# One maximum for both halves of a query's keys, and 1/sum applied to the attention's output

## The chip, the cores and the metric

The kernel runs on one core of a Trainium2 chip. The metric is the device time of one execution in microseconds, as the median of several runs. A profile of one execution gives a trace: when each instruction started and ended on each engine. TensorE (PE, with its weight loads PEld), VectorE (DVE), ScalarE (ACT), GpSimd (POOL) and the DMA queue of SyncE (SP) work side by side and wait for each other by semaphores.

## The reference

Block-causal attention over 8 batches, 8 heads, 576 positions and 64 dimensions, followed by a gated feed-forward layer with a depthwise convolution:

```python
scores = (q @ k^T) / 8
scores = where(pos_i // 64 >= pos_j // 64, scores, -1e9)
attn = exp(scores - max(scores, axis=-1))
attn = attn / (sum(attn, axis=-1) + 1e-9)
x = attn @ v                       # heads side by side: [8, 576, 512]
h = relu(x @ w_in)                 # w_in [512, 1024]
conv = sum over k of conv_w[k] * h shifted by k - 1      # 3 taps along the sequence
out = (h * sigmoid(conv)) @ w_out  # w_out [1024, 512]
```

All is float32. The kernel keeps the precision of the two large products by splitting each operand in a high and a low part (`x`: hi and lo, `wih`/`wil`, `woh`/`wol`, `gh`/`gl`), and runs three matmuls for each product.

## The kernel before

**Pairs and visits.** Attention works on pairs of heads, 32 pairs in all, four to a batch. The first batch is visited twice (part A: query blocks 0 to 3, part B: blocks 4 to 8), all other pairs once (part None, blocks 0 to 8), which makes 36 visits, here called pair 0 to 35. After the four pairs of a batch its feed-forward runs in two halves (`ffn`): first products on line 998, second products on line 1064.

**Scores.** A query block of 64 rows sees `b + 1` key blocks. The kernel lays a block's scores out so that the four quadrants of 32 partitions hold two groups of 32 queries times two halves of the keys: quadrants 0 and 1 (and 2 and 3) have the same queries and different halves of their keys. Only so do 64 queries fill 128 partitions. The blocks of a pair go in sets, `((8, 5), (7, 6), (4, 3, 2, 1, 0))`; each set takes two PSUM banks. TensorE makes the scores (line 852), VectorE the maximum of each row over its half (line 865, stored negated in `st`), ScalarE the exponential with that maximum as bias and the row sum as a by-product (line 870), all into `p`.

**Joining the halves.** Each half has its own maximum, so `merge` joins them: four copies of 32 partitions (ScalarE line 886 for two quadrants, GpSimd through the helper on line 506 for two) bring the other half's maximum and sum; then a subtraction (L893), an exponential of it (L896), two small operations (L899, L903) and a reciprocal (L907) give a factor for each row. GpSimd multiplies all of P with it (`norm`, line 919), in two operations for each block.

**PV.** VectorE transposes P in 32 x 32 blocks (line 938) into `ptw`, TensorE multiplies it with V (line 951, 144 matmuls in a full pair), and the output, transposed (dimensions on partitions, queries along the row), is evicted as a high part by ScalarE (line 965) and a low part by VectorE (line 968) straight from PSUM.

**Order.** Nothing is scheduled when the kernel is built: `Plan.op` numbers the operations, and the list `ORDER` gives the order in which they are issued, which is the order of each engine's queue, the DMA queue of SP included. `BANKS` says which PSUM bank each operation uses. `FILLS` puts filler matmuls (line 1159, `operation:bank:count`, result unused) ahead of named operations on TensorE. All three lists were computed beforehand from estimated costs of the operations; the numbers in the calls of `pl.op` (durations, target times) have no effect on the code that runs.

Of the kernel before, what the change touches and what calls it, by code (L numbers as in the profile page):

```python
# [195 lines left out]
"""  # L196

FILLS = """
46:0:17 32:0:9 62:0:2 127:0:6 58:0:17 257:4:4 165:3:10 566:0:7 28:2:14 391:6:2 295:0:5 495:3:2 431:5:1 755:0:7 719:0:6
# [995 lines left out]
```

## Time and profile before

| | |
|---|---|
| median of 3 runs | 693.44 us (692.34 to 694.99) |
| the profiled execution's own time | 692.34 us |
| its span (first to last instruction) | 690.2 us |
| mean granted TensorE clock | 0.998 |
| busy, share of the span | PE 97%, PEld 81%, DVE 84%, ACT 77%, POOL 65% |

The span is 2.1 us shorter than the time of the same execution. Matmuls are pipelined, so a busy TensorE is not one that works at its peak rate; how close it is shows in the time from one matmul to the next.

### The profile page before, as it was taken

To read this page: it belongs to the slowest core of one execution; us is meant where nothing else is said; L and a number is where in the kernel's file an instruction comes from. 1 tells how busy PE (TensorE), PEld (TensorE's weight loads), DVE (VectorE), ACT (ScalarE), POOL (GpSimd) and SP (SyncE) were. 2 spreads that over 40 slices of the span, in tenths; PEclk is the share of its full clock that TensorE was granted. 3 is DMA by queue.
4 is the path that set the end of the run, shared out by engine and by line. 5 is a ranking of instruction groups with operands and counts; after the bars stand their busy time and mean duration, and the time that the engine had idled before them with its cause. 6 is when DMAs were issued, how large, how long until landed. Compare 5 with 4: busy or idle time off the path is not lost.

```text
span 690.2 us, 29902 instructions
## 1 busy us (share of the span) xinstructions
PE 669.7 (97%) x12090; PEld 562.0 (81%) x12090; DVE 581.8 (84%) x1409; ACT 531.6 (77%) x2004; POOL 449.0 (65%) x918
## 2 busy tenths in 40 slices
PE   8979999999999999999999999999999999999998
PEld 6666768868979788887888889787988788888986
DVE  5778999998799878989799989988899978886662
ACT  5867888888798768887878879876789777884663
POOL 1564676886677955687668765778567765676242
PEclk9999999999999999999999999999999999999999
DMA  6885565417434342434343434424443352212002
GB/s 168 182 197 111 110 140 86 76 39 145 96 62 85 70 104 53 86 79 96 59 80 76 91 78 81 71 65 75 95 77 70 72 123 44 53 37 83 2 0 77
DMA packets 238542, 58.59 MB, mean 85 GB/s; under 512 B 228524, under 2 KB 232900, under 8 KB 238404
## 3 DMA queue, kind: packets, MB, share of 16 engines
q1 hardware_dynamic: 237060, 55.76, 39.5%
q8 instruction: 95, 1.56, 1.0%
q10 hardware_dynamic: 1344, 0.92, 0.4%
q14 instruction: 43, 0.35, 0.2%
HBM read 47.21 MB, written 9.44 MB: 82 GB/s over the span
## 4 chain that ended last, share of the span: by engine, by line
PE 72%; DVE 9%; ACT 6%; POOL 4%; issue 4%; DMA 2%; SPq 2%; DVEq 0%; POOLq 0%; ACTq 0%
PE banks L1064 25%; PE banks L998 24%; PE banks L951 11%; PE banks L852 10%; POOL p L919 3%; ACT p L870 3%; DVE ptw L938 2%; DVE st L865 2%; PE banks L691 1%; PE banks L1159 1%; SPq L538 1%; DMA t<-in_moe_conv_w_dram 1%; DVE t L1031 1%; ACT t L1015 1%; POOL gl L1038 1%
## 5 line engine op out<-in xcount | busy, mean ns | idle before, releaser
L919 POOL TENSOR_SCALAR p<-p,st 128x224 f32<-128x224 f32 (+8 forms) x576 | 262.9, 475 | 59.4 <-DVE st L907 52.2
L870 ACT ACTIVATE p<-banks,st 128x288 f32<-128x288 f32 (+8 forms) x576 | 220.6, 400 | 40.2 <-DVE st L865 27.5
L998 PE MATMUL banks<-x,wih 128*128 128x290 f32 (+3 forms) x1024 | 186.3, 301 | 1.2 <-ACT x L965 1.2
L998 PEld LDWEIGHTS banks<-x,wih 128*128 128x128 f32 x1024 | 154.8, 189 | 11.0 <-issue 3.0
L1038 POOL TENSOR_TENSOR gl<-t,gh 128x289 fp32r<-128x289 f32 (+3 forms) x128 | 106.4, 841 | 56.1 <-ACT gh L1035 45.7
L938 DVE STREAM_TRANSPOSE ptw<-p 128x576 f32<-128x576 f32 (+8 forms) x272 | 127.8, 495 | 12.8 <-POOL p L919 4.6
L865 DVE TENSOR_REDUCE st<-banks 128x2 f32<-128x64 f32 (+8 forms) x288 | 124.8, 471 | 12.0 <-PE banks L852 11.5
L870 ACT ACTIVATION_READ_ACCUMULATOR p<-banks,st 128x1 f32 x576 | 121.8, 211 | 0.0
L1064 PE MATMUL banks<-woh,gh 128*128 128x512 f32 (+1 forms) x296 | 119.0, 402 | 0.8 <-ACT h L1012 0.8
L1064 PE MATMUL banks<-woh,gl 128*128 128x512 f32 (+1 forms) x296 | 115.3, 389 | 0.3 <-POOL gl L1038 0.3
L1064 PE MATMUL banks<-wol,gh 128*128 128x512 f32 (+1 forms) x296 | 115.3, 390 | 0.0
L998 PE MATMUL banks<-x,wil 128*128 128x288 f32 (+3 forms) x512 | 105.8, 299 | 0.0
L852 PE MATMUL banks<-kT,qT 64*32 64x128 f32 (+8 forms) x4464 | 102.4, 302 | 3.2 <-issue 1.2
L852 PEld LDWEIGHTS banks<-kT,qT 64*32 64x32 f32 x4464 | 71.5, 105 | 31.4 <-issue 10.0
L951 PEld LDWEIGHTS banks<-ptw,vn 64*32 64x32 f32 x4608 | 81.1, 105 | 18.2 <-issue 5.4
L951 PE MATMUL banks<-ptw,vn 64*32 64x160 f32 (+8 forms) x4608 | 91.8, 296 | 4.2 <-issue 2.5
L1019 DVE SCALAR_TENSOR_TENSOR t<-h,cw,t 128x289 f32<-128x289 f32 (+3 forms) x128 | 74.8, 590 | 19.1 <-ACT t L1015 18.7
L506 POOL TENSOR_SCALAR st<-st 32x16 f32<-32x16 f32 (+2 forms) x136 | 34.0, 250 | 84.4 <-ACT p L870 32.1
L998 PEld LDWEIGHTS banks<-x,wil 128*128 128x128 f32 x512 | 82.1, 189 | 3.2 <-issue 1.1
L1023 DVE SCALAR_TENSOR_TENSOR t<-h,cw,t 128x288 f32<-128x288 f32 (+3 forms) x128 | 75.0, 594 | 1.6
L1015 ACT ACTIVATE t<-h,cw 128x289 f32<-128x289 f32 (+3 forms) x128 | 67.5, 536 | 5.9 <-POOL gl L1038 3.4
L1031 DVE SCALAR_TENSOR_TENSOR t<-t,h 128x289 f32<-128x289 f32 (+3 forms) x128 | 66.3, 529 | 5.7 <-ACT t L1028 5.1
(93 smaller groups left out, 797.2 us busy)
## 6 DMA issues: line engine op xcount, KB each, us to landing
vn<-in_v_dram SPq DMA_DIRECT2D x128, 144.0 KB, 3.6
out_dram<-stage SPq DMA_DIRECT2D x35, 256.0 KB, 2.6
kT<-in_k_dram SPq DMA_DIRECT2D x112, 72.0 KB, 3.0
qT<-in_q_dram SPq DMA_DIRECT2D x112, 72.0 KB, 2.9
x<-in_moe_w_out_dram SPq DMA_DIRECT2D x8, 512.0 KB, 4.8
gl<-in_moe_w_in_dram SPq DMA_DIRECT2D x4, 512.0 KB, 4.7
vxa<-in_v_dram SPq DMA_DIRECT2D x8, 128.0 KB, 5.3
gh<-in_moe_w_in_dram SPq DMA_DIRECT2D x2, 512.0 KB
```

What stands on the lines that cost most here:

```text
L852: nc.tensor.matmul(both(sb)[32 * quad:32 * quad + 32, h, o:o + w].rearrange("p (u n) -> p u n", n=32), t["q"].ap[r, 64 * b + 32 * g:64 * b ...
L865: nc.vector.tensor_reduce(out=st.ap[:, c:c + 2], in_=both(sb)[:, :, off:off + w], op=ALU.max, axis=AX.X, negate=True)
L870: nc.scalar.activation(out=pt.ap[:, h, :], in_=both(sb)[:, h, off:off + w], func=AF.Exp, bias=st.ap[:, c:c + 1], accum_out=st.ap[:, n + c: ...
L919: nc.gpsimd.tensor_scalar(out=pt.ap[:, h, :], in0=pt.ap[:, h, :], scalar1=st.ap[:, 5 * n + c:5 * n + c + 1], scalar2=0.0, op0=ALU.mult, op ...
L938: nc.vector.transpose(pt.ap[:, :, b:b + rise * b + 1:rise, :], x.ap.rearrange("p h (u n) -> p h u n", n=32))
L951: nc.tensor.matmul(both(vb)[o:o + 32, g, 32 * (lo - b0):32 * (b1 - b0)].rearrange("p (b n) -> p b n", n=32), vat(u, h)[r, 32 * y:32 * y + ...
L998: nc.tensor.matmul(fb.ap[:, 0:n2], wt[:, c, fs], xs[c][xi].ap[:, x0:x0 + n2], start=(n + c - c0 == 0), stop=(n + c - c0 == 3 * NCC - 1))
L1015: nc.scalar.activation(out=t.ap[:, 0:no], in_=hb.ap[:, own:own + no], func=AF.Copy, scale=cw[:, NFC + f:NFC + f + 1])
L1019: nc.vector.scalar_tensor_tensor(out=t.ap[:, i0:no], in0=hb.ap[:, own + i0 - 1:own + no - 1], scalar=cw[:, f:f + 1], in1=t.ap[:, i0:no], o ...
L1023: nc.vector.scalar_tensor_tensor(out=t.ap[:, 0:i1], in0=hb.ap[:, own + 1:own + 1 + i1], scalar=cw[:, 2 * NFC + f:2 * NFC + f + 1], in1=t.a ...
L1038: nc.gpsimd.tensor_tensor(out=gbuf[1].ap[:, f, carry:carry + no], in0=t.ap[:, 0:no], in1=gbuf[0].ap[:, f, carry:carry + no], op=ALU.subtract)
L1064: nc.tensor.matmul(fb.ap[:, 0:cut], gbuf[a].ap[:, f, cs], w[:, f, ds], start=(f == 0 and n == 0), stop=(f == NFC - 1 and n == 2))
```

## The change

The exponentials wait for one maximum for both halves. For each set, after the maxima, four copies of 32 partitions bring the other half's maximum (two on ScalarE, two on GpSimd), VectorE takes the minimum of the two negated maxima, and the exponentials use that as bias. P of both halves is then on the same scale and is no longer multiplied: `merge` and `norm` are gone.

The sums are joined once for each pair, in `inverse`: four copies on GpSimd bring the other half's sum, VectorE adds the two (and 1e-9), four more copies on GpSimd lay the sums out so that each partition of `it` has the value of one query for each block, VectorE takes the reciprocal, and a transpose whose source is repeated 32 times along the row spreads it over partitions into `rb`, in the layout of PV's output.

After PV, VectorE multiplies the output from PSUM with `rb` into `rb`; ScalarE copies that as the high part of x, and GpSimd subtracts to make the low part. The PSUM banks of PV are then free after one operation instead of two.

`ORDER`, `BANKS` and `FILLS` are new: 5,016 operations instead of 5,272, and 78 filler matmuls instead of 109. In the new order the eight loads of the first batch's V on SP stand ahead of two of the weight loads and four of the q/k loads that were ahead of them. The matmuls of scores, PV and feed-forward are the same.

```diff
-    MERGE = {"A": ((0,),), "B": ((0, 1), (2,)), None: ((0, 1), (2,))}
+    SWACT, SUMACT = (0, 1), ()
+    LOWPOOL = True
@@ FILLS
-46:0:17 32:0:9 62:0:2 127:0:6 58:0:17 257:4:4 165:3:10 566:0:7 28:2:14 391:6:2 295:0:5 495:3:2 431:5:1 755:0:7 719:0:6
+32:0:14 105:0:10 127:2:5 168:3:7 170:3:1 99:3:3 235:2:1 46:0:2 535:0:1 547:0:13 379:6:10 721:7:5 433:3:1 483:0:1 1107:2:4
@@ stage_s, for each set
+            sw = swaps(lambda r, cs=cs: st.ap[r, 1, cs, :], lambda r, cs=cs: st.ap[r, 0, cs, :], SWACT, t0 + 1.0, ms, [st], len(blocks))
+            def top(cs=cs):
+                nc.vector.tensor_tensor(out=st.ap[:, 2, cs, :], in0=st.ap[:, 0, cs, :], in1=st.ap[:, 1, cs, :], op=ALU.min)
...
-                                             bias=st.ap[:, c:c + 1], accum_out=st.ap[:, n + c:n + c + 1])
+                                             bias=st.ap[:, 2, c, h:h + 1], accum_out=st.ap[:, 3, c, h:h + 1])
-    def merge(st, n, cols, es, pq, t0):
...
-                    nc.gpsimd.tensor_scalar(out=pt.ap[:, h, :], in0=pt.ap[:, h, :], scalar1=st.ap[:, 5 * n + c:5 * n + c + 1], scalar2=0.0,
-                                            op0=ALU.mult, op1=ALU.add)
+    def inverse(st, nb, sums, at):
+        sw = swaps(lambda r: st.ap[r, 4, :, :], lambda r: st.ap[r, 3, :, :], SUMACT, at, sums, [st], nb)
...
+            nc.vector.scalar_tensor_tensor(out=st.ap[:, 5, :, :], in0=st.ap[:, 3, :, :], scalar=EPS, in1=st.ap[:, 4, :, :], op0=ALU.add, op1=ALU.add)
...
+                    pool_copy(it.ap[64 * h:64 * h + 64, g, :], st.ap[64 * g:64 * g + 64, 5, :, h])
...
+            nc.vector.reciprocal(it.ap, it.ap)
...
+            nc.vector.transpose(rb.ap[:, :, 0:nb, :], it.ap.unsqueeze(3).broadcast_to([P, 2, nb, 32]))
@@ stage_pv
+        def mul():
+            nc.vector.tensor_tensor(out=rb.ap[:, :, 0:b1 - b0, :], in0=both(vb)[:, :, 0:w].rearrange("p g (b n) -> p g b n", n=32),
+                                    in1=rb.ap[:, :, 0:b1 - b0, :], op=ALU.mult)
         def evh():
-            nc.scalar.activation(out=dst(0), in_=got(), func=AF.Copy)
+            nc.scalar.activation(out=out(0), in_=rb.ap[:, :, 0:b1 - b0, :], func=AF.Copy)
         def evl():
-            nc.vector.tensor_tensor(out=dst(1), in0=got(), in1=dst(0), op=ALU.subtract)
+            eng = nc.gpsimd if LOWPOOL else nc.vector
+            eng.tensor_tensor(out=out(1), in0=rb.ap[:, :, 0:b1 - b0, :], in1=out(0), op=ALU.subtract)
```

## Rows read from the trace of the kernel before

**Rows 1.** The page's head, of the whole run: busy us of each engine with its share of the span and its instructions.

```profile
span 690.2 us, 29902 instructions
PE 669.7 (97%) x12090; PEld 562.0 (81%) x12090; DVE 581.8 (84%) x1409; ACT 531.6 (77%) x2004; POOL 449.0 (65%) x918
```

**Rows 2.** The windows view: stretch and its length in us, then busy us (and instructions) of PE, PEld, DVE, ACT and POOL, the mean granted TensorE clock, the DMA engines' share, GB/s.

```profile
0.00:40.00 40.00, 36.94 (x578) 26.66 (x579) 26.75 (x89) 28.57 (x117) 16.64 (x51) 1.00 0.81 182
40.00:45.00 5.00, 5.00 (x151) 4.01 (x150) 4.41 (x11) 3.92 (x17) 3.83 (x9) 1.00 1.01 274
45.00:50.00 5.00, 1.68 (x45) 0.92 (x30) 2.42 (x11) 2.48 (x8) 1.45 (x3) 0.95 0.73 124
50.00:55.00 5.00, 5.00 (x23) 4.33 (x24) 4.13 (x10) 2.29 (x6) 4.29 (x6) 0.71 0.67 126
55.00:90.00 35.00, 34.02 (x594) 23.80 (x593) 32.18 (x75) 28.95 (x94) 19.65 (x39) 1.00 0.55 116
90.00:133.00 43.00, 41.32 (x773) 33.16 (x771) 41.49 (x104) 37.59 (x140) 29.31 (x56) 1.00 0.56 102
```

**Rows 3.** The chain of work that ended last, in order of time: start us, length us, what (xcount of instructions).

```profile
38.70 3.40 PE banks L1159 x14
60.09 0.47 PE banks L688 x2
60.55 0.86 PE banks L691 x2
200.54 2.77 PE banks L951 x128
378.37 2.77 PE banks L852 x128
382.97 6.32 PE banks L1064 x27
633.43 2.77 PE banks L951 x128
636.19 14.53 PE banks L998 x108
```

**Rows 4.** The same chain in the start of the run.

```profile
14.70 2.18 ACT p L870 x14
32.03 2.89 DMA vxa<-in_v_dram
45.17 3.31 issue
```

**Rows 5.** The groups of instructions by line, of what the change takes away: line, engine, operation, out<-in, shape, count | busy us, mean ns of one | idle us before them, and what ended most of it.

```profile
L919 POOL TENSOR_SCALAR p<-p,st 128x224 f32<-128x224 f32 (+8 forms) x576 | 262.9, 475 | 59.4 <-DVE st L907 52.2 <-DVE st L899 1.9 <-DMA kT<-in_k_dram 1.2
L506 POOL TENSOR_SCALAR st<-st 32x16 f32<-32x16 f32 (+2 forms) x136 | 34.0, 250 | 84.4 <-ACT p L870 32.1 <-issue 28.4 <-DVE t L1023 7.2
L886 ACT ACTIVATE st<-st 32x16 f32<-32x16 f32 (+2 forms) x136 | 29.2, 216 | 2.8
L899 DVE SCALAR_TENSOR_TENSOR st<-st 128x8 f32<-128x8 f32 (+1 forms) x68 | 17.0, 249 | 5.2 <-ACT st L896 4.7
L893 DVE TENSOR_TENSOR st<-st 128x8 f32<-128x8 f32 (+1 forms) x68 | 16.8, 247 | 12.2 <-ACT st L886 4.8 <-POOL st L506 4.2 <-issue 1.3
L903 DVE SCALAR_TENSOR_TENSOR st<-st 128x8 f32<-128x8 f32 (+1 forms) x68 | 16.6, 244 | 1.2
L896 ACT ACTIVATE st<-st 128x8 f32<-128x8 f32 (+1 forms) x68 | 14.1, 208 | 16.4 <-DVE st L893 15.8
L907 DVE RECIPROCAL st<-st 128x8 f32<-128x8 f32 (+1 forms) x68 | 13.4, 197 | 1.3
```

**Rows 6.** Groups by line with each shape apart, for the sizes that stand nearest to the new operations (the rows of L1012 and L1035 are groups by line with all shapes).

```profile
L938 DVE STREAM_TRANSPOSE ptw<-p 128x576 f32<-128x576 f32 x32 | 24.2, 755 | 1.0 <-POOL stage L595 0.6 <-POOL st L506 0.4
L968 DVE TENSOR_TENSOR x<-banks,x 128x576 fp32r<-128x576 f32 x28 | 20.7, 740 | 15.2 <-ACT x L965 15.1
L865 DVE TENSOR_REDUCE st<-banks 128x2 f32<-128x192 f32 x32 | 11.0, 344 | 0.1
L938 DVE STREAM_TRANSPOSE ptw<-p 128x64 f32<-128x64 f32 x28 | 6.1, 218 | 0.6 <-POOL p L919 0.5
L1038 POOL TENSOR_TENSOR gl<-t,gh 128x289 fp32r<-128x289 f32 x56 | 46.7, 844 | 15.1 <-ACT gh L1035 14.5
L965 ACT ACTIVATE x<-banks 128x576 fp32r<-128x576 f32 x28 | 18.3, 653 | 11.5 <-PE banks L951 11.2
L1035 ACT ACTIVATE gh<-t 128x289 fp32r<-128x289 f32 (+3 forms) x128 | 55.1, 443 | 14.7 <-DVE t L1031 9.8 <-POOL gh L506 3.3 <-DVE st L899 1.2
L1012 ACT ACTIVATE h<-banks 128x290 f32<-128x290 f32 (+3 forms) x128 | 50.6, 407 | 17.5 <-PE banks L998 16.4 <-DVE t L1031 0.6
```

**Rows 7.** The timeline of VectorE and GpSimd at two places (start us, us, engine, line, operation, out<-in).

```profile
255.89 0.40 POOL L919 TENSOR_SCALAR p<-p,st 128x160 f32<-128x160 f32 x1
255.83 0.17 DVE L893 TENSOR_TENSOR st<-st 128x8 f32<-128x8 f32 x1 [0.41 <-POOL st L506]
270.08 0.81 POOL L1038 TENSOR_TENSOR gl<-t,gh 128x287 fp32r<-128x287 f32 x1 [1.13 <-DVE st L893]
270.13 0.78 DVE L899 SCALAR_TENSOR_TENSOR st<-st 128x8 f32<-128x8 f32 x1
```

**Rows 8.** Who waited for whom in the whole run, one pair of lines: us in total, times, longest us.

```profile
PEld banks L852 <- ACT p L870: 3.8, 11, 0.5
```

More of the change, by code (lines that the diff above doesn't have):

```diff
@@ L829, in c_tile, with spread, swaps, swap @@
         return sum(max(2 * 0.000836 * w + more, least) for w in widths)
+    RBN = two
+    def spread(blocks, b0):
+        x = sorted(b - b0 for b in blocks)
+        return slice(x[0], x[-1] + 1, x[1] - x[0] if len(x) > 1 else 1)
+    def swaps(to, fr, acts, at, deps, bufs, n):
+        res = []
+        for quad in range(4):
+            act = quad in acts
+            def swap(quad=quad, act=act):
+                a, b = to(slice(32 * (quad ^ 1), 32 * (quad ^ 1) + 32)), fr(slice(32 * quad, 32 * quad + 32))
+                if act:
+                    nc.scalar.activation(out=a, in_=b, func=AF.Copy)
+                else:
+                    pool_copy(a, b)
+            res.append(pl.op(ACT if act else POOL, 0.23 if act else 0.26, swap, at, deps=deps, bufs=bufs))
+        return res
     def stage_s(ops, at, part, step):
         t, ready = ops
-        pq, stats, done = {}, [], []
+        b0, b1 = SPAN[part]
+        nb = b1 - b0
+        st = two([P, 6, nb, 2], F32, f"st{nb}")
+        pq, done, sums = {}, [], []
         for z, blocks in enumerate(SETS[part]):
-            m = next(i for i, x in enumerate(MERGE[part]) if z in x)
-            if z == MERGE[part][m][0]:
-                cols = [(b, h) for y in MERGE[part][m] for b in SETS[part][y] for h in range(2)]
-                n = len(cols)
-                st = two([P, 6 * n], F32, f"st{n}")
-                es = []
             t0 = at + step * z
@@ L861, in stage_s, with mx @@
                 pq[b] = held(f"p{b}", [pfix[b]], 1, firstq) if b > 3 else two([P, 2, w], F32, f"p{b}")
-                c = cols.index((b, 0))
-                def mx(sb=sb, off=off, w=w, c=c, st=st):
-                    nc.vector.tensor_reduce(out=st.ap[:, c:c + 2], in_=both(sb)[:, :, off:off + w], op=ALU.max, axis=AX.X, negate=True)
+                def mx(sb=sb, off=off, w=w, c=b - b0):
+                    nc.vector.tensor_reduce(out=st.ap[:, 0, c, :], in_=both(sb)[:, :, off:off + w], op=ALU.max, axis=AX.X, negate=True)
@@ L867, in stage_s @@
                 ms.append(pl.op(DVE, c_dve(2 * w), mx, t0 + 0.6, deps=[o], bufs=sb + [st]))
+            cs = spread(blocks, b0)
+            sw = swaps(lambda r, cs=cs: st.ap[r, 1, cs, :], lambda r, cs=cs: st.ap[r, 0, cs, :], SWACT, t0 + 1.0, ms, [st], len(blocks))
+            def top(cs=cs):
+                nc.vector.tensor_tensor(out=st.ap[:, 2, cs, :], in0=st.ap[:, 0, cs, :], in1=st.ap[:, 1, cs, :], op=ALU.min)
+            o = pl.op(DVE, 0.075, top, t0 + 1.3, deps=sw, bufs=[st])
+            x = 0
@@ L868, in stage_s, with ex @@
+            for b, off in zip(blocks, offs):
+                w = 32 * (b + 1)
+                es = []
                 for h in range(2):
-                    def ex(sb=sb, h=h, off=off, w=w, c=c + h, st=st, n=n, pt=pq[b]):
+                    def ex(sb=sb, h=h, off=off, w=w, c=b - b0, pt=pq[b]):
                         nc.scalar.activation(out=pt.ap[:, h, :], in_=both(sb)[:, h, off:off + w], func=AF.Exp,
-                                             bias=st.ap[:, c:c + 1], accum_out=st.ap[:, n + c:n + c + 1])
@@ new lines, in ex, with add, rec, go @@
+                                             bias=st.ap[:, 2, c, h:h + 1], accum_out=st.ap[:, 3, c, h:h + 1])
+                    es.append(pl.op(ACT, c_act(w, True, True, True) + 0.01, ex, t0 + 1.5 + 0.4 * x, deps=[o], bufs=sb + [st, pq[b]]))
+                    x += 1
+                sums += es
+                done.append((b, es, t0 + 2.5 + 0.4 * x))
+        return pq, (done, inverse(st, nb, sums, t0 + 5.0))
+    def inverse(st, nb, sums, at):
+        sw = swaps(lambda r: st.ap[r, 4, :, :], lambda r: st.ap[r, 3, :, :], SUMACT, at, sums, [st], nb)
+        it = two([P, 2, nb], F32, f"it{nb}")
+        rb = RBN([P, 2, NBK, 32], F32, "rb")
+        def add():
+            nc.vector.scalar_tensor_tensor(out=st.ap[:, 5, :, :], in0=st.ap[:, 3, :, :], scalar=EPS, in1=st.ap[:, 4, :, :], op0=ALU.add, op1=ALU.add)
+        def rec():
+            nc.vector.reciprocal(it.ap, it.ap)
+        o = pl.op(DVE, 0.075, add, at + 0.3, deps=sw, bufs=[st])
+        mv = []
+        for h in range(2):
+            for g in range(2):
+                def go(h=h, g=g):
+                    pool_copy(it.ap[64 * h:64 * h + 64, g, :], st.ap[64 * g:64 * g + 64, 5, :, h])
+                mv.append(pl.op(POOL, 0.26, go, at + 0.5, deps=[o], bufs=[st, it]))
+        o = pl.op(DVE, 0.12, rec, at + 1.0, deps=mv, bufs=[it])
+        def tr():
+            nc.vector.transpose(rb.ap[:, :, 0:nb, :], it.ap.unsqueeze(3).broadcast_to([P, 2, nb, 32]))
+        return rb, pl.op(DVE, c_dve(64 * nb) + 0.025, tr, at + 1.2, deps=[o], bufs=[it, rb])
@@ L956, in stage_pv, with out @@
         w = 32 * (b1 - b0)
-        def dst(j):
+        def out(j):
             return xx[j].ap[:, 64 * b0:64 * b1].rearrange("p (b g n) -> p g b n", g=2, n=32)
-        def got():
-            return both(vb)[:, :, 0:w].rearrange("p g (b n) -> p g b n", n=32)
+        def mul():
+            nc.vector.tensor_tensor(out=rb.ap[:, :, 0:b1 - b0, :], in0=both(vb)[:, :, 0:w].rearrange("p g (b n) -> p g b n", n=32),
+                                    in1=rb.ap[:, :, 0:b1 - b0, :], op=ALU.mult)
         def evh():
-            nc.scalar.activation(out=dst(0), in_=got(), func=AF.Copy)
+            nc.scalar.activation(out=out(0), in_=rb.ap[:, :, 0:b1 - b0, :], func=AF.Copy)
         def evl():
-            nc.vector.tensor_tensor(out=dst(1), in0=got(), in1=dst(0), op=ALU.subtract)
-        e = pl.op(ACT, c_act(2 * w), evh, at + 3.0, deps=[o], bufs=vb + [xx[0]])
-        es = [pl.op(DVE, c_dve(2 * w), evl, at + 3.3, deps=[e], bufs=vb + [xx[0], xx[1]])]
+            eng = nc.gpsimd if LOWPOOL else nc.vector
+            eng.tensor_tensor(out=out(1), in0=rb.ap[:, :, 0:b1 - b0, :], in1=out(0), op=ALU.subtract)
+        e = pl.op(DVE, c_dve(2 * w), mul, at + 3.0, deps=[o, inv], bufs=vb + [rb])
+        e = pl.op(ACT, c_act(2 * w, False), evh, at + 3.5, deps=[e], bufs=[xx[0], rb])
+        if LOWPOOL:
+            es = [pl.op(POOL, c_pool(2 * w, True), evl, at + 4.0, deps=[e], bufs=[xx[0], xx[1], rb])]
+        else:
+            es = [pl.op(DVE, c_dve(2 * w, two_in=True), evl, at + 4.0, deps=[e], bufs=[xx[0], xx[1], rb])]
         ready(es)
```

51 lines of the change are left out of this document (6 added, 45 removed), and 329 rows, old and new, of the table ORDER.

## The prediction, before the change was run

> **What bounds the kernel now.** I read the page first. One engine stands above the others: TensorE is busy 669.7 of 690.2 us (97%), against 84% on VectorE, 77% on ScalarE and 65% on GpSimd [rows 1]. Busy is not the same as dense, so I next took the chain that ended last and read from it how long one matmul takes where they follow each other without a hole [rows 3]: 14.53/108 = 0.1345 us for the first FFN product (L998), 6.32/27 = 0.234 for the second (L1064), 2.77/128 = 0.0216 for scores (L852), 0.43 for L691, 0.235 for L688, and 3.40/14 = 0.243 for a filler matmul (L1159). A whole PV of 144 matmuls takes 2.77 us, 0.0192 each.
>
> With these rates I counted the PE operations in ORDER and FILLS, cut at two PVs whose start the trace shows: that of pair 12 at 200.54 us and that of pair 35, the last, at 633.43 [rows 3].
> Up to 200.54: 324 of L998 (43.6), 120 of L1064 (28.1), 1440 of scores (31.1), 1408 of PV (27.0), 17 weight splits of 0.235 + 0.87 + 0.235 (22.8), 109 fillers (26.5): 179.1 us of work, 21.4 lost.
> From there to 633.43: 1044, 624, 3168 and 3312: 418.4 of work in 432.9, 14.5 lost (3%).
> From 633.43 to the end: 53.5 of work, 3.3 for the last eviction and store.
> So the middle is nearly dense matmul. What can be won lies mostly in the first 200 us: the fillers and the loss there.
>
> The windows show what that stretch waits for [rows 2]. To 45 us the DMA engines are the full ones (0.81, then 1.01). Between 45 and 50 PE does 1.68 us. From 55 to 133 VectorE is busy 73.7 of 78 us, so it binds there nearly as much as PE.
>
> **The change part by part.**
> *PE.* The matmuls are the same. FILLS falls from 109 to 78 matmuls: 31 x 0.243 = -7.5 us. The new ORDER shifts work between the stretches: by the same rates 162.5 up to pair 12's PV, 420.7 up to pair 35's, 60.4 after it. With the losses of before, 162.5 + 21.4 + 420.7 + 14.5 + 60.4 + 3.3 = 682.8 against 690.2. The bounds: 0, if the place of the 31 fillers stays empty, and the whole 7.5, since the fillers lie on the chain where it passes them [rows 3]. I take the whole, because the eight V loads now stand ahead of two weight loads and four q/k loads in SP's order, and the first PV waited 2.89 us for such a load (vxa) [rows 4].
>
> *GpSimd.* 576 multiplications of P go, 262.9 us in all, 8.2 per full pair, and 136 swaps of st, 34.0 us [rows 5]. In come 200 swaps of the maxima, 144 of the sums and 144 moves into it, 488 x 0.25 = 122 us by the swap's row, and 36 subtractions of the low half of x. Its nearest row is the two-input subtraction of L1038, 844 ns for 289 columns: 576 columns make 1.68 us, all 36 some 54 us [rows 6]. GpSimd falls from 449 to about 328 us. It is not the bound, so this is worth 0 by itself, hidden under PE.
>
> *VectorE.* Out go four small operations of 68 each, 17.0 + 16.8 + 16.6 + 13.4 = 63.8 us [rows 5]. In come 100 minima and 36 additions of about 0.248 (33.7), 36 reciprocals of 0.197 (7.1), and 36 broadcast transposes. The trace has no transpose with a repeated source; below it lies half the plain one, above it twice, and I take the plain one, 755 ns at 576 columns [rows 6], some 25 us with the narrow ones. The multiplication from PSUM takes the place of the subtraction from PSUM, 740 ns [rows 6]. Net +2 us, between -11 and +27; in the 78 us where VectorE binds that is 0.2, between -1 and +3. Taken as 0.
>
> *The shared reads of VectorE and GpSimd.* A small two-input VectorE operation took 0.78 us at 270.13, under a GpSimd subtraction of 0.81 that ended with it; beside a one-input multiplication, at 255.83, such an operation took 0.17 [rows 7]. So the 36 new subtractions, 1.68 us each, are the kind that holds VectorE, and the 576 multiplications were mostly not. That speaks against the change: if each of the 36 holds one two-input operation for 0.6 us, VectorE gains 22 us over the run, 2.5 in its binding stretch. The Trainium skill (GPSIMD Engine Reference, Key points) says that GpSimd's contention is with VectorE instructions that have two SBUF inputs or run in a two-port mode; the two rows agree, and by it the sum would be the same 22. The four small operations that go were held in the same way: 0.08 above 0.17 in the mean of three of them, 204 in all, 16 us [rows 5, 7], while 136 small two-input ones come. Between -2 and +3 on the path; taken as 0.
>
> *ScalarE.* 136 swaps become 200 (64 x 0.215 = +13.8), 68 small exponentials go (-14.1) [rows 5], and 36 evictions read SBUF instead of PSUM (nearest rows: 443 ns for 289 columns from SBUF, 407 for 290 from PSUM [rows 6], so +0.04 each, +1.3): +1 us of 532, taken as 0.
>
> *The new wait.* An exponential used to wait for the maximum of its set; now for maximum, swap (0.25) and minimum (0.25), so a set holds its score banks about 0.5 us longer, and the ScalarE queue behind the first exponential waits with it. ORDER puts other ScalarE work between swap and first exponential in 81 of 100 sets. PE waits for these banks 3.8 us in the whole run [rows 8]. In return P is ready for the transposes without the 8.2 us of multiplications. The new ORDER spends this: the PE work between a full pair's last scores and its PV falls from 23.5 to 13.3 us on the mean, and the least from 13.1 to 6.3. For the set of five blocks the new chain needs 1.7 (five maxima, 0.34 for the middle one) + 0.5 + 10 x 0.31 (seven narrow exponentials took 2.18) + 0.2 for the last transpose, 5.5 us [rows 4, 6]: just covered. Bounds 0 and, at 0.5 for each of 100 sets, +50; I take 0, nearest to the 3.8 that PE waits now.
>
> *The end of a batch.* x comes after 0.74 + 0.65 + 1.68 instead of 0.65 + 0.74 [rows 6], 1.7 us later. After the last PV, ORDER still has three second products of batch 6 (2.1 us) and products that need only the other pairs: 0. Uncovered it would be 1.7 x 9 = 15.
>
> **Sum.** 690.2 - 7.4 = 682.8 span. The profiled execution took 692.34, 2.1 more than its span, so 684.9; the median of before, 693.44, is 1.1 above it: **686.0 us**, its own range 680 to 690. A difference under 0.5% (3.5 us) can't be told from no change here.
>
> **The rivals.**
> *A, the start gets shorter by more.* The early V loads remove the wait at 32 us, and with it the 3.31 us idle at 45.17 [rows 4]; half of the 21.4 lost goes: 672.1 span, 675 us. For it: DMA share 1.01 just before. Against: the trace names nothing for the 3.31 us.
> *B, the start is bound elsewhere.* The loads and VectorE (73.7 of 78) set when weights are ready, and the 31 filler places stay empty: 690 span, 693 us.
> *C, the spent cover is missing.* This one ends slower. Six full pairs have under 9 us between last scores and PV. If the maximum-swap-minimum-exponential chain takes 2 us more than the rows make it, because the swaps stand behind 1.68 us subtractions in GpSimd's queue, PE stops 2 us at each of the six; it decides from 1.2 us each, where the 7.4 are gone. With 2 us, 694.8; with the same happening for 1 us in half of the other 22 pairs, 706 span. Say 698 to 709 us.
> *D, idle in place of fillers, and a slower clock.* After the 3.31 us idle the granted clock was 0.95 and 0.71 of full speed, on the mean of two windows of 5 us, so partly at the lower of its two levels, 1.2 instead of 2.4 GHz [rows 2, 4]: 5 x 0.29 + 5 x 0.05 = 1.7 us lost. If the 7.5 us of fillers turn into four such holes, 690.3 + 6.8 = 697 span, 700 us. The Trainium skill (TensorE: Matmul & The Clock Gate, section HAM oscillation) names idle gaps that bring the half clock back as a cost paid each time, and feeding PE as the cure, so it speaks against fewer fillers; the one hole here agrees.
>
> **How the numbers follow.** My forecast 0.47, A 0.17, B 0.16, C 0.14, D 0.06. Faster 0.47 + 0.17 = 0.64, same 0.16, slower 0.20. From 672 (A with a little more) to 700 (D, and C's first case) leaves out little over 1 in 10.
>
> **What would show it.** Right: 78 matmuls of the filler line; PE's L998 and L1064 rates unchanged; pair 35's PV near 619; GpSimd busy near 330, VectorE near 580. A: pair 12's PV before 175 us instead of about 184. B: PE's idle time before 133 us grows by 7. C: waits of PV for the transposes, and of ScalarE for the minimum, each over 20 us. D: a granted clock under 1.0 outside one stretch. Wrong altogether if VectorE's busy time rises by 20 us or more, that is, if the broadcast transpose or the held operations cost twice what I took.

## The result: slower, with all the work that was to go gone

The changed kernel takes 702.38 us (median of 4 runs, 701.78 to 702.87) against 693.67 for the kernel before on the same chip: ratio 1.0125, 95% interval 1.0104 to 1.0147. The prediction was 686.0 in a range of 672 to 700. It is wrong in sign and outside its range.

The profiled execution of the changed kernel took 701.78 us, with a span of 699.8. Line numbers have moved: scores are L862 (852 before), PV L952 (951), first products L1005 (998), second products L1071 (1064), fillers L1166 (1159), exponentials L890 (870). The head of its page, against [rows 1]:

```profile
span 699.8 us, 29716 instructions
PE 665.2 (95%) x12059; PEld 556.9 (80%) x12059; DVE 574.9 (82%) x1345; ACT 535.2 (76%) x2000; POOL 325.3 (46%) x730
q8 instruction: 95, 1.56, 1.0%
```

Every engine but ScalarE has less to do than before, TensorE too, and the span is 9.6 us longer. The last line is the queue that brings TensorE's instructions: packets, MB, share of 16 DMA engines. It becomes the main witness below.

The groups of what came in, by line (columns as in [rows 5]):

```profile
L498 POOL TENSOR_SCALAR st<-st 32x18 f32<-32x18 f32 (+4 forms) x344 | 85.1, 247 | 164.8 <-DVE st L874 93.1 <-ACT p L890 45.5 <-DVE t L587 3.7
L498 POOL TENSOR_SCALAR it<-st 64x9 f32<-64x9 f32 (+2 forms) x144 | 37.9, 263 | 26.3 <-DVE st L906 16.4 <-DVE st L881 0.8 <-PE banks L862 0.5
L837 ACT ACTIVATE st<-st 32x4 f32<-32x4 f32 (+3 forms) x200 | 41.2, 207 | 44.3 <-DVE st L874 41.5
L881 DVE TENSOR_TENSOR st<-st 128x4 f32<-128x4 f32 (+3 forms) x100 | 22.6, 227 | 17.7 <-ACT st L837 7.7 <-POOL st L498 4.8 <-issue 3.6
```

And the three operations of a full pair whose cost had no row of their own before, each shape apart:

```profile
L971 POOL TENSOR_TENSOR x<-rb,x 128x576 fp32r<-128x576 f32 x28 | 40.6, 1451 | 21.6 <-ACT x L967 21.1
L922 DVE STREAM_TRANSPOSE rb<-it 128x576 f32<-128x576 f32 x28 | 21.6, 770 | 0.5
L963 DVE TENSOR_TENSOR rb<-banks,rb 128x576 f32<-128x576 f32 x28 | 21.0, 749 | 8.8 <-PE banks L952 8.2
```

A transpose whose source is repeated costs what the plain one of the same size costs (770 ns, 755 before [rows 6]); the multiplication from PSUM costs what the subtraction from PSUM cost (749 against 740 [rows 6]). All of these are near their estimates. So I looked where TensorE's time went. The chain that ended last, in order of time (as [rows 3]):

```profile
186.38 2.58 PE banks L952 x121
277.92 11.44 PE banks L1071 x48
349.59 1.48 issue
635.24 2.77 PE banks L952 x126
641.09 6.93 PE banks L1005 x52
```

Pair 12's PV starts at 186.2 (its first record lies just ahead of the chain's 186.38), 14.3 us earlier than before. Pair 35's PV starts at 635.2, 1.8 us later than before [rows 3]. So what was won in the first 200 us is lost in the middle. The matmuls are no slower there: 11.44/48 = 0.238 and 6.93/52 = 0.133 us each, as before. TensorE stands still instead. The windows of 200 to 633 us (columns as in [rows 2]), after:

```profile
200.00:633.00 433.00, 416.11 (x7935) 354.81 (x7919) 367.54 (x850) 342.30 (x1330) 201.43 (x455) 1.00 0.38 75
```

and before:

```profile
200.00:633.00 433.00, 427.53 (x8149) 366.67 (x8148) 382.78 (x919) 344.58 (x1345) 306.21 (x631) 1.00 0.37 76
```

TensorE is idle for 16.9 us there instead of 5.5, at full clock, with every other engine less busy. The view of waits says for whom it waits. After (us in total, times, longest us):

```profile
PE banks L862 <- issue: 10.9, 14, 1.5
PE banks L952 <- issue: 9.8, 12, 1.9
PE banks L862 <- ACT t L1035: 2.1, 1, 2.1
```

Before:

```profile
PE banks L951 <- issue: 5.8, 5, 3.3
PE banks L852 <- issue: 1.2, 2, 0.7
```

For nobody. "issue" is idle time in which an engine waited for nothing that the profile shows, and all but the whole rise is there: 7.0 to 20.7 us, all of it ahead of the small attention matmuls. With a last gap of 0.6 us ahead of a first product it is 21.2 after, against 7.0 before. All of TensorE's waits for other engines together are 9.0 us before and 9.1 after, so what my rival C was about did not come to TensorE.

**What the stops have in common.** The instruction queue brought 95 packets in 1.56 MB, 16 KB each. TensorE executed 12,059 matmuls and 12,059 weight loads, 24,118 instructions, so a packet holds some 254 of them, about 128 matmuls with their weight loads. I numbered the matmul records of the changed kernel and marked the stops: they stand at numbers 345, 725, 1232, 1487, 1741, 2121, 2504, 2757, 3520, 3902 and so on, whose distances (380, 507, 255, 254, 380, 383, 253, 763, 382) are all multiples of about 127.2. That is one packet's worth: with the 159 semaphore and drain instructions of the same queue the trace has 24,277 instructions, 94.8 times 256, and 12,059/94.8 = 127.2. Numbered over that whole queue, all 27 stops of the changed kernel, and all 7 of the kernel before (its 3.31 us at 45.17 [rows 4] among them), fall on the same place of their 256, to within one instruction, and each ends 1.25 to 1.7 us after a packet of the instruction queue has landed. In the traces of all the kernels run here it is 231 of 234 such gaps of over 0.15 us. Here is one stop in the timeline of TensorE (start us, us, engine, line, operation, idle before):

```profile
344.78 1.04 PE L862 MATMUL banks<-kT,qT 64*32 64x256 f32 x32
345.62 2.82 PE L952 MATMUL banks<-ptw,vn 64*32 64x288 f32 x144
348.39 1.20 PE L862 MATMUL banks<-kT,qT 64*32 64x160 f32 x79
351.06 0.21 PE L862 MATMUL banks<-kT,qT 64*32 64x32 f32 x1 [1.48 <-issue]
```

The set of scores is cut between its 79th and its 80th matmul, where no operation begins and no semaphore is waited for: 32 + 144 + 79 = 255 matmuls after the last large product. By the trace's records of the queue, a packet started at 348.45, 0.8 us after TensorE had entered the block before (at 347.67), and landed at 349.59; TensorE went on at 351.06, 1.5 us later. At the other stops it goes on 1.25 to 1.7 us after such a landing. 128 attention matmuls last 2.5 to 2.8 us, less than this round takes; a block with large products in it lasts up to 22 us and mostly hides it (4 of the 27 stops follow such a block).

**Theory 1**, then: TensorE's instructions come in blocks of 16 KB, a block takes over 3 us to bring, and blocks of attention matmuls alone are used up faster. The new ORDER has more of these in a row. Counted in the trace, before had 3 uninterrupted runs of 256 or more attention matmuls (800 matmuls in all), after has 14 (3,680); blocks that are attention to over 97% number 21 or 22 before, as the borders are drawn, and 30 after. **Rivals:** theory 2, that the place in the instruction stream has no part and the stops come from something else in the new order; theory 3, that GpSimd's new subtractions hold VectorE and so the middle.

### The profile page after: what moved, and what is told of

Its sections match the earlier page's. It is cut to its first block, busy times and chain, and to the rows that moved or that the text cites. A ratio compares the mean times of both kernels' runs of the same rounds, so it can differ in the third digit from the quotient of the medians.

```text
span 699.8 us, 29716 instructions
## 1 busy us (share of the span) xinstructions
PE 665.2 (95%) x12059; PEld 556.9 (80%) x12059; DVE 574.9 (82%) x1345; ACT 535.2 (76%) x2000; POOL 325.3 (46%) x730
## 3 DMA queue, kind: packets, MB, share of 16 engines
q8 instruction: 95, 1.56, 1.0%
## 4 chain that ended last, share of the span: by engine, by line
PE 83%; ACT 6%; DVE 4%; issue 4%; DMA 1%; POOL 0%; ACTq 0%; DVEq 0%
PE banks L1005 27%; PE banks L1071 27%; PE banks L862 13%; PE banks L952 11%; ACT p L890 3%; PE banks L683 2%; PE banks L1166 1%; DVE st L874 1%; DMA gh<-in_moe_w_in_dram 1%; DVE ptw L939 1%; PE banks L680 1%; ACT t L1022 1%; DVE t L1030 1%; DVE t L1026 1%; DMA out_dram<-stage 1%
## 5 line engine op out<-in xcount | busy, mean ns | idle before, releaser
L890 ACT ACTIVATE p<-banks,st 128x128 f32<-128x128 f32 (+8 forms) x576 | 220.8, 398 | 19.7 <-DVE st L881 17.9
L1005 PE MATMUL banks<-x,wih 128*128 128x290 f32 (+3 forms) x1024 | 185.6, 300 | 1.0 <-issue 0.6
L1005 PEld LDWEIGHTS banks<-x,wih 128*128 128x128 f32 x1024 | 154.3, 189 | 10.9 <-issue 4.4
L498 POOL TENSOR_SCALAR st<-st 32x18 f32<-32x18 f32 (+4 forms) x344 | 85.1, 247 | 164.8 <-DVE st L874 93.1
L874 DVE TENSOR_REDUCE st<-banks 128x2 f32<-128x128 f32 (+8 forms) x288 | 125.8, 475 | 16.5 <-PE banks L862 14.4
L939 DVE STREAM_TRANSPOSE ptw<-p 128x128 f32<-128x128 f32 (+8 forms) x272 | 128.0, 497 | 13.4 <-ACT p L890 7.0
L890 ACT ACTIVATION_READ_ACCUMULATOR p<-banks,st 128x1 f32 x576 | 121.2, 210 | 0.0
L1071 PE MATMUL banks<-woh,gh 128*128 128x512 f32 (+1 forms) x296 | 119.9, 405 | 0.1
L862 PE MATMUL banks<-kT,qT 64*32 64x224 f32 (+8 forms) x4464 | 106.2, 302 | 13.4 <-issue 10.2
L1071 PE MATMUL banks<-wol,gh 128*128 128x512 f32 (+1 forms) x296 | 116.4, 393 | 0.0
L1071 PE MATMUL banks<-woh,gl 128*128 128x512 f32 (+1 forms) x296 | 116.3, 393 | 0.0
L862 PEld LDWEIGHTS banks<-kT,qT 64*32 64x32 f32 x4464 | 71.5, 105 | 41.8 <-issue 24.0
L1005 PE MATMUL banks<-x,wil 128*128 128x290 f32 (+3 forms) x512 | 104.8, 297 | 0.0
L952 PE MATMUL banks<-ptw,vn 64*32 64x96 f32 (+8 forms) x4608 | 93.0, 296 | 10.5 <-issue 9.8
L952 PEld LDWEIGHTS banks<-ptw,vn 64*32 64x32 f32 x4608 | 82.1, 105 | 24.8 <-issue 14.6
L1026 DVE SCALAR_TENSOR_TENSOR t<-h,cw,t 128x289 f32<-128x289 f32 (+3 forms) x128 | 69.4, 549 | 30.1 <-ACT t L1022 29.9
L1005 PEld LDWEIGHTS banks<-x,wil 128*128 128x128 f32 x512 | 81.4, 188 | 3.1 <-issue 1.3
L1030 DVE SCALAR_TENSOR_TENSOR t<-h,cw,t 128x287 f32<-128x287 f32 (+3 forms) x128 | 73.8, 585 | 1.6
L837 ACT ACTIVATE st<-st 32x4 f32<-32x4 f32 (+3 forms) x200 | 41.2, 207 | 44.3 <-DVE st L874 41.5
L1035 ACT ACTIVATE t<-t 128x287 f32<-128x287 f32 (+3 forms) x128 | 55.9, 446 | 17.4 <-DVE t L1030 17.0
```

The costliest lines, as they stand in the source:

```text
L498: nc.gpsimd.tensor_scalar(out=dst, in0=src, scalar1=1.0, scalar2=0.0, op0=ALU.mult, op1=ALU.add)
L862: nc.tensor.matmul(both(sb)[32 * quad:32 * quad + 32, h, o:o + w].rearrange("p (u n) -> p u n", n=32), t["q"].ap[r, 64 * b + 32 * g:64 * b ...
L874: nc.vector.tensor_reduce(out=st.ap[:, 0, c, :], in_=both(sb)[:, :, off:off + w], op=ALU.max, axis=AX.X, negate=True)
L890: nc.scalar.activation(out=pt.ap[:, h, :], in_=both(sb)[:, h, off:off + w], func=AF.Exp, bias=st.ap[:, 2, c, h:h + 1], accum_out=st.ap[:, ...
L939: nc.vector.transpose(pt.ap[:, :, b:b + rise * b + 1:rise, :], x.ap.rearrange("p h (u n) -> p h u n", n=32))
L952: nc.tensor.matmul(both(vb)[o:o + 32, g, 32 * (lo - b0):32 * (b1 - b0)].rearrange("p (b n) -> p b n", n=32), vat(u, h)[r, 32 * y:32 * y + ...
```

## The experiments

Times are medians; "before" was run again beside them on the same chip each time: 693.18 (17 runs) for the first four, 692.47 (15) for the next four, 692.81 (25) for the last four. In the shifted kernels only filler matmuls are replaced, whose results nobody uses.

**The attention sets moved apart.** 95 feed-forward products are moved in ORDER to stand between adjacent attention sets. One of the lines touched (498 to 500 and 474 are such products):

```diff
-451 708 712 448 730 692 495 734 765 732 496 497 461 771 474 452 729 498 696 388 499 697 337 500 735 462 745 700 338 453 715 736 986 414 746 415 454
+451 708 712 448 730 692 495 734 765 732 496 497 461 771 452 729 696 388 697 337 735 462 745 474 498 499 500 700 338 453 715 736 986 414 746 415 454
```

> The changed kernel, with 95 of the 1,064 feed-forward products moved in TensorE's order so that they stand between scores and PVs that followed each other without a break; nothing else differs, and all other queues keep their order. Theory 1 (instruction blocks): TensorE gets its instructions in packets of 16 KB, 256 instructions, and a block of nothing but small attention matmuls is executed sooner than the next block is there, so that TensorE stops for nothing that the profile shows as a wait. The blocks with over 97% attention matmuls fall from 30 to 12. Expected 688 us (684 to 692), idle with releaser 'issue' ahead of score and PV matmuls from 61 us (PE and PEld rows together) to under 30. Theory 2 (the spent cover, rival C of the prediction: maximum, swap, minimum, exponential come too late): the products that stand between do not make that chain shorter, 702 us (699 to 706).

Measured: 715.97 us, ratio 1.0342 (1.0317 to 1.0366). Both expectations missed. TensorE's waits in this kernel:

```profile
PE banks L952 <- issue: 4.2, 8, 0.9
PE banks L862 <- ACT p L890: 4.0, 8, 0.8
PE banks L862 <- issue: 3.8, 4, 2.2
PE banks L1005 <- ACT stage L1079: 3.3, 4, 1.4
```

and its windows:

```profile
0.00:55.00 55.00, 47.57 (x818) 33.05 (x826) 38.35 (x116) 38.33 (x151) 24.73 (x76) 0.94 0.78 174
55.00:133.00 78.00, 72.64 (x1402) 56.04 (x1387) 72.12 (x169) 63.24 (x211) 39.79 (x90) 0.98 0.49 99
```

The stops on attention lines did go, from 20.7 to 8.0 us. But moved products are moved past their banks and inputs: after 61 us the waits for other engines rose from 3.4 to 17.8 us, the changes between small and large matmuls from 142 to 206, and the clock was 0.94 and 0.98 of full speed in the two stretches, 55 x 0.06 + 78 x 0.02 = 4.9 us lost (the changed kernel has 1.00 and 0.98 there, 1.6 us lost). So this shows that parting attention removes most of the stops, and says nothing for the time: it changed too much at once.

**The low half of x on VectorE again**, which takes the 36 new subtractions from GpSimd.

```diff
-    LOWPOOL = True
+    LOWPOOL = False
```

> The changed kernel with the low half of x made by VectorE instead of GpSimd (36 subtractions, in the same place of the order). Theory 3 (shared reads): the 36 subtractions on GpSimd hold two-input operations of VectorE, so without them VectorE's other rows get shorter and the time falls by 5 to 10 us, to 692 to 697. Theory 1: TensorE's order is the same, 702 us (699 to 706), as VectorE has 36 x 0.7 = 25 us more to do, which is not on the path.

Measured: 706.01 us, ratio 1.0212 (1.0176 to 1.0247), at the upper end of theory 1's 699 to 706 and far from theory 3's 692 to 697. Its page:

```profile
PE 668.4 (95%) x12059; PEld 556.6 (79%) x12059; DVE 588.0 (84%) x1381; ACT 535.5 (76%) x2000; POOL 281.9 (40%) x694
```

The stops stay (22.1 us of "issue"), so theory 3 is out. VectorE gets 36 subtractions of 689 ns, 24.8 us, and its four groups of two-input operations (L881, L1026, L1030, L1038) fall from 227.7 to 221.1: being held by GpSimd cost 6.6 us in the run, where I had allowed 22.

**A shift by 48 matmuls.** In the first filler group, which starts at 1 us, 10 of 14 fillers are replaced by 58 tiny matmuls (29 calls of two), so that all that follows stands 48 places further in the stream. Nothing else is changed.

```diff
         def go():
-            for _ in range(k):
+            if x is blank:
+                tiny = blank[0:64, 0:32].bitcast(F32)
+                for _ in range(29):
+                    nc.tensor.matmul(slot[0:32, 0:32], tiny, tiny, start=True, stop=True, skip_group_check=True)
+            for _ in range(4 if x is blank else k):
```

> The changed kernel with 10 of the first 14 filler matmuls, which run before any data has come, replaced by 29 tiny ones (58 matmul records): the order and all work stay the same, but every later instruction of TensorE lies 48 matmuls (96 instructions) further on in its block of 256. Theory 1: other stretches of the order now fill a block alone; counted from the order, with a block needing 3.35 us at least, the loss falls by 6 us: 696 us (693 to 699), and the stops move to other places. Theory 2: 702 us (700 to 704), stops at the same instructions.

Measured: 691.95 us, 0.9993 of the kernel before (0.9974 to 1.0012), that is 10.4 us less than the changed kernel, for a few tiny matmuls, and 1 us below theory 1's range of 693 to 699. The stop shown above, in this kernel:

```profile
338.92 1.04 PE L862 MATMUL banks<-kT,qT 64*32 64x256 f32 x32
339.75 2.82 PE L952 MATMUL banks<-ptw,vn 64*32 64x288 f32 x144
342.54 0.72 PE L862 MATMUL banks<-kT,qT 64*32 64x160 f32 x31
344.09 0.73 PE L862 MATMUL banks<-kT,qT 64*32 64x128 f32 x49 [0.84 <-issue]
```

The same 80 scores are now cut after 31 instead of 79: the stop moved back by 48 matmuls, the shift. It is also shorter, and "issue" over the run fell from 21.2 to 14.3.

**The same shift by 128**, one whole packet (69 calls), the control for the edit itself.

> Control of the run before it: 69 tiny matmuls (138 records) instead of the same 10 fillers, so that everything lies one whole block (128 matmuls) further on and the blocks hold the same instructions as in the changed kernel. Both theories: 702 us (700 to 704); theory 1 also says that the stops come at the same instructions as in the changed kernel.

Measured: 702.22 us, ratio 1.0148 (1.0125 to 1.0172): the changed kernel's time again. The same place:

```profile
351.90 1.20 PE L862 MATMUL banks<-kT,qT 64*32 64x160 f32 x79
354.58 0.21 PE L862 MATMUL banks<-kT,qT 64*32 64x32 f32 x1 [1.49 <-issue]
```

Cut after 79, for 1.49 us, as in the unshifted kernel. A shift by a whole packet restores stop and time, a shift by part of one moves both. That is theory 1, and theory 2 can't give it.

**The kernel before, shifted by 49** (13 of its first 17 fillers replaced by 31 calls).

> The kernel before with the same edit as the half shift of the changed kernel: 13 of its first 17 filler matmuls, which run before any data has come, replaced by 31 tiny ones (62 records), so that everything lies 49 matmuls further on in its block of 256 instructions. Theory 1 (instruction blocks): counted from the order, the blocks of nothing but attention matmuls go from 22 to 20 and the loss by 2 to 3 us: 691 us (688 to 694). If the gain of the half shift lay in the edit itself (fewer fillers at the start) and not in the place of the blocks, this one would gain the same 10 us: 683.

Measured: 699.43 us, ratio 1.0099 (1.0066 to 1.0133). I expected 2 us less and got 7 more. "issue" rose from 7.0 to 10.5. So the kernel before hangs on its place as well, and it stood at a good one.

**Fewer blocks of attention alone.** In the kernel shifted by 48, 13 such blocks are parted by some 0.8 us of feed-forward products; in the kernel before, 17. One line of each ORDER:

```diff
-1695 1666 1692 1397 1441 1736 1667 1810 1398 1442 1699 1409 1443 1698 1444 1694 1735 1668 1445 1669 1693 1446 1700 1697 1455 1696 1456 1447 1427 1737
+1441 1442 1443 1695 1666 1692 1397 1736 1667 1810 1398 1699 1409 1698 1444 1694 1735 1668 1445 1669 1693 1446 1700 1697 1455 1696 1456 1447 1427 1737
...
-849 862 871 995 872 1009 994 1056 873 1039 991 1012 874 1040 826 1011 1105 875 1010 850 837 1048 876 863 1013 1047 1063 838 1055 1041 864 1064 1046
+849 862 871 995 1009 994 1056 1039 991 1012 1040 826 1011 1105 872 873 874 875 1010 850 837 1048 876 863 1013 1047 1063 838 1055 1041 864 1064 1046
```

> The half shift of the changed kernel, and in 13 of the blocks that still hold nothing but attention matmuls, after 130 us, two or three feed-forward products (0.8 us) moved in from next to the block. Theory 1: the stops fall by about 0.7 us at each of the 13, 9 us; each new change between the two shapes of matmul costs some of it (327 instead of 234 ns was seen between a second product and scores in the kernel before), so 4 to 6 us: 687 us (684 to 691). Theory 2: 692 us or more.

> The kernel before, without a shift, with two or three feed-forward products moved into 17 of the blocks that hold nothing but attention matmuls, after 130 us. Theory 1: the same loss is in this kernel too, though smaller (stops of 3.7 us after 61 us): 690 us (687 to 694). If only the changed kernel has it: 693 to 697.

Measured: 697.20 us (1.0073, 1.0046 to 1.0100) and 696.42 us (1.0067, 1.0038 to 1.0095): both slower than what they were made from, so by the time alone neither forecast of theory 1 came true. After 61 us the "issue" gaps fell as expected, from 11.1 to 5.1 and from 3.7 to 1.6, and the other waits rose by more, from 3.0 to 12.6 and from 6.2 to 9.8. In the first, TensorE now waits for the exponentials:

```profile
PE banks L862 <- ACT p L890: 5.5, 8, 1.6
```

The expectations took the moves for free, and they aren't: ORDER places these products where their inputs and banks are ready.

**The stop by itself.** Behind all of the work of the kernel before stand 512 calls of a matmul of 32 columns and 512 of one of 256, each call making two matmuls, with no waits among them and results unused.

```diff
+    side = wol[:, 0, 0:256].bitcast(F32)
+    for n in (32, 256):
+        for i in range(512):
+            h, quad = i % 2, i // 2 % 4
+            r = slice(64 * h, 64 * h + 64)
+            nc.tensor.matmul(psum[h][32 * quad:32 * quad + 32, 0:n], side[r, 0:32], side[r, 0:n], start=True, stop=True, skip_group_check=True)
```

> The kernel before with two runs of 512 unused matmuls behind its last one, when almost no transfer is under way: first 512 of 64 x 32 weights on 32 columns, then 512 of the same weights on 256 columns (two records each, 8 blocks of instructions each). Theory 1: the thin run is held to some 3 us for each 128 records, 8 x 3 = 24 us, with stops of over 0.5 us at every 128th record and none between; the wide run takes over 3.5 us for 128 records by itself and has no stop. Without a limit on instructions the thin run takes 1024 x 0.010 to 0.017 = 10 to 17 us, evenly.

Measured, in a single run: 28.0 us for the narrow ones, where theory 1 had 24. The chain of this stretch:

```profile
689.79 1.99 PE banks L1171 x124
691.78 2.51 issue
694.29 1.55 PE banks L1171 x80
695.84 2.47 issue
698.31 1.55 PE banks L1171 x82
699.86 2.20 issue
702.05 1.55 PE banks L1171 x83
...
717.31 30.37 PE banks L1171 x1052
```

In the timeline each of the pieces of 1.55 us is 128 matmuls. TensorE executes 128 narrow matmuls in at most 1.55 us and stands for 2.20 to 2.51, seven times over: a block takes 3.74 to 4.02 us however short its work. The wide ones have no stop, at 3.8 us for 128. And the transfers are nearly silent meanwhile:

```profile
690.00:717.00 27.00, 11.06 (x967) 10.12 (x950) 0.00 (x0) 0.21 (x1) 0.00 (x0) 0.57 0.05 18
```

The DMA engines are busy to 0.05 there, so it is not a crowded queue that makes a block slow. It is not a slow clock either: the granted clock was 1.00 until after the first and longest stop had begun, and that block took 3.83 us. From 694.3 to 717.3 us, TensorE being idle more than half of the time, it was 0.50, the lower of its two levels; the 1.55 us and the 3.74 to 4.02 of the later blocks are at that level. The page of this kernel has 111 instruction packets against 95: 16 more for 2,048 matmuls, 128 to a packet.

The Trainium skill (Runtime: NRT & Kernel Launch, section Instruction fetch mechanics) says that an engine's instructions are refilled in blocks of 16 KiB, 256 instructions, and that crossing into the next block is mostly hidden. The first half agrees with 16 KB and 256 instructions a packet here; the second does not hold for TensorE where the matmuls are short: 2.2 to 2.5 us of each 3.74 to 4.02 in this run.

**The change apart from its place.** Both kernels at two further places each, by the same edit (17 and 47 calls after, 19 and 52 before), to see what the change is worth on the mean of places.

> The changed kernel; in the first filler group 10 of the 14 filler matmuls are replaced by 34 tiny ones of 32 columns (results unused, as a filler's), so that all later matmuls of TensorE stand 24 places further in its instruction stream. Theory 1 (TensorE stops where its stream passes from one block of 16 KB of instructions to the next after a block of attention matmuls only, and the change itself is worth about -7 us outside of these stops): counting blocks that are short of 3.1 us in the order gives 15.6 us of such stops against 18.7 unshifted, so about 699 us (695 to 701); the span without the gaps ended by 'issue' is 674 to 679 us, as in the changed kernel and the two shifts of it. Theory 2 (the place in the stream has no part; the 692 us of the shift by 48 came from the replaced fillers): 692 us, as there.

> The changed kernel, shifted by 84 matmuls in the same way (94 tiny ones for 10 fillers). Theory 1: 15.7 us of short blocks against 18.7, so about 699 us (695 to 702); span without the gaps ended by 'issue' 674 to 679 us. Theory 2: 692 us.

> The kernel before, shifted by 25 matmuls (13 of the 17 fillers of the first group replaced by 38 tiny ones). Theory 1: 11.9 us of short blocks against 13.3, about 692 us, but the shift by 49 missed in this by 8 us, so only 690 to 700; the span without the gaps ended by 'issue' is the sharper test: 682 to 686 us, about 7 above the changed kernel's. Theory 2: the same time as the shift by 49, 699 us.

> The kernel before, shifted by 91 matmuls (104 tiny ones for 13 fillers). Theory 1: 11.9 us of short blocks against 13.3, 690 to 700 us; span without the gaps ended by 'issue' 682 to 686 us. Theory 2: 699 us.

Measured, with all the shifts; span and "issue" are those of the one profiled execution of each, which can lie some 3.5 us off the median. One value of "issue" is good to 3 or 4 us: at the same place the changed kernel had 21.2 and 25.3 (0 and 128), and the kernel before 7.0 and, in the run with the narrow matmuls, 10.1 ahead of these.

| kernel, shift | median us (ratio to before, interval) | span | "issue" of TensorE | the rest of the span |
|---|---|---|---|---|
| after, 0 | 702.38 (1.0104 to 1.0147) | 699.8 | 21.2 | 678.6 |
| after, 24 | 699.11 (1.0061 to 1.0119) | 693.8 | 16.9 | 676.9 |
| after, 48 | 691.95 (0.9974 to 1.0012) | 687.9 | 14.3 | 673.6 |
| after, 84 | 693.34 (0.9969 to 1.0021) | 687.9 | 12.5 | 675.4 |
| after, 128 | 702.22 (1.0125 to 1.0172) | 702.5 | 25.3 | 677.2 |
| before, 0 | 693.67 | 690.2 | 7.0 | 683.2 |
| before, 25 | 697.75 (1.0050 to 1.0095) | 693.6 | 11.7 | 681.9 |
| before, 49 | 699.43 (1.0066 to 1.0133) | 694.7 | 10.5 | 684.2 |
| before, 91 | 699.41 (1.0059 to 1.0131) | 696.0 | 12.9 | 683.1 |

The shift by 24 came at 699.1, where theory 1 had 699 and theory 2 692. The shift by 84 came at 693.3, nearer to theory 2's 692 than to my 699: counting short blocks gives no good size for each place. The times of the two shifts of the kernel before (697.8 and 699.4) lie in theory 1's wide range and near theory 2's 699, and tell nothing apart. The last column is the sharper test, and there the kernels fall in two groups, as expected: 673.6 to 678.6 (mean 676.3) for the changed kernel wherever it stands, 681.9 to 684.2 (mean 683.1) for the kernel before. Outside of the stops the change, with its new order and fewer fillers, is worth -6.8 us.

The stops take that back. Over the four different places (0, 24, 48, 84 and 0, 25, 49, 91) they cost 16.2 us on the mean after and 10.5 before: 5.7 us more, which goes with the new order's longer runs of attention; from values that are good to 3 or 4 us each, the size is rough. By the same values the other 8.5 of the 14.2 us by which the two kernels differ is place: the changed kernel stands 5.0 above its mean, the kernel before 3.5 below its own. The times say the same: the means over the four places are 696.7 after and 697.6 before, no difference that four places each can show, and the changed kernel as it was lies 5.7 above its mean, the kernel before 3.9 below its own. None of the kernels run here was faster than the kernel before by more than its interval.

## Why the prediction was wrong

**The failed step** is in the sum, in five words: "With the losses of before". I took TensorE's loss in each stretch over unchanged, the 14.5 us of the middle among them. Measured in the same stretches, with my own work terms:

| stretch | predicted | measured | more | of it "issue" more than before |
|---|---|---|---|---|
| to pair 12's PV | 162.5 + 21.4 = 183.9 | 186.2 | 2.3 | 6.2 - 3.8 = 2.4 |
| to pair 35's PV | 420.7 + 14.5 = 435.2 | 449.0 | 13.8 | 15.0 - 3.3 = 11.7 |
| to the end | 60.4 + 3.3 = 63.7 | 64.6 | 0.9 | 0 |

The sum of 682.8 missed the span by 17.0, and 14.1 of that is idle time with no releaser. A loss is not a property of a stretch of time: it belongs to the order of the work and to the place of that work in the instruction stream, and this change replaces the one and moves the other. The place is luck: nothing in the prediction weighed it, and at the shifts by 48 and 84 the same change would have read as no difference from the kernel before. The rows of before did show the thing itself. PE's rows of the view of waits had "issue" as the largest entry (5.8 and 1.2 us), and I read only the row of the exponentials [rows 8], since I was looking for waits on other engines. The chain of the start had 3.31 us of "issue" [rows 4], which I called unnamed and used for rival A; it is a stop like the others. The sign that I had named, pair 35's PV near 619, came at 635.2.

**A row read wrongly.** The 2.89 us of vxa [rows 4], which I took for the first PV's wait, are the load's own time on the chain. TensorE waited 0.6 us for it:

```profile
PE banks L951 <- DMA vxa<-in_v_dram: 0.6, 1, 0.6
```

So this was no ground for counting the whole 7.5 us of the fillers. The term came out near its size all the same, since the 2.3 us more to pair 12's PV are "issue"; no run tells why.

**The work terms** were right. 78 fillers ran (64 and 14); the rates are unchanged; the rest column gives -6.8 for the change where the sum had -7.4.

**GpSimd and VectorE.** GpSimd 325.3 us for a predicted 328, VectorE 574.9 for about 584 by the sum: the broadcast transpose and the minima came as taken, the subtraction on GpSimd cost 1451 ns instead of 1.68 us at 576 columns, and the shared reads cost 6.6 us instead of 22. None of this was on the path, as said.

**ScalarE** 535.2, 3.6 more than before; I had +1.

**"The new ORDER spends this."** The prediction counted that the work between a pair's last scores and its PV falls from 23.5 to 13.3 us, and asked only whether the exponentials still fit in. They do: TensorE waits 0.6 us for exponentials and its weight loads 2.8, no more than the 3.8 of before [rows 8]. But scores and PV closer together fit with more attention matmuls in one run (14 runs of 256 or more for 3). That the one causes the other is argued, not tested.

**The rivals.** A (pair 12 before 175 us): 186. B (idle time of TensorE before 133 us up by 7): from 9.0 to 11.7, by the windows. C had the sign and the time (698 to 709), by another cause: no wait of PV for transposes stands among TensorE's larger waits, and ScalarE's wait for the minimum, 17.9 us where C wanted over 20, hardly reached TensorE, which waited 0.6 us for exponentials. D (idle in place of fillers and a slower clock): the granted clock was 0.96 of full speed over 90 to 133 us, 43 x 0.04 = 1.7 us, and 1.00 in all other stretches that I read. The kernel before lost 1.7 us in the same way at 45 to 55 us [rows 2], so nothing is left for D.

**What would have been needed:** a rival "TensorE stops with no releaser", with a price. By before's own rows one of 5 such stops cost 1.2 us on the mean ahead of PV (5.8/5, with one of 3.3 among them); 14 long runs for 3, at one such stop each, is 11 x 1.2 = 13 us, a rough price. ORDER was there to count the runs in.

**Still open:** why a block needs over 3 us, since the packet itself takes 0.9 to 1.6 and TensorE goes on only 1.25 to 1.7 after it has landed; and how many blocks are held ahead. No run here tells that apart. The shifts of the kernel before had no control by a whole packet.

## What to carry to other kernels

Where a kernel issues long runs of short matmuls, look for stops of TensorE ended by "issue" and number its matmuls. Here all but 3 of 234 lay at multiples of one distance, 256 instructions or some 127 matmuls, and there the order of the work, the number of instructions and even a few fillers changed the time by over 1%. Two versions whose instruction counts differ should then be compared at several places in the stream before an edit gets the credit or the blame: here the same change reads as +1.25% with both kernels as they were, and as -1.1% with both shifted by about 48 matmuls (691.95 of 699.43 us, ratios 0.9993 and 1.0099 to the same kernel). A loss in the profile of before is carried to another order only with its cause.

## What the runs showed of the hardware

- TensorE took one block of 256 instructions in 3.74 to 4.02 us in a quiet stretch (narrow run), where their execution takes 1.55 at a granted clock of 0.50; the first such block, at 1.00, took 3.83. In the changed kernel blocks of attention alone lasted 3.4 us on the mean (30 blocks), 2.7 of them with TensorE at work.
- 58 tiny matmuls in place of 10 fillers (a shift by 48) made the changed kernel 10.4 us faster; 138 in place of the same 10 (a shift by 128) left it as it was.
- A change from large to small matmuls costs TensorE some 0.09 us, read in the trace of before from the distance of two matmuls: 327 ns from a second product to a score where two second products stand 234 apart, 225 for 134 from a first product (medians). Products put between attention sets pay this each time.
- A VectorE transpose whose source is repeated 32 times along the row took 770 ns for 576 columns, the plain one 755.
